# Feed-forward products whose moving operand is read alternately from two halves of a row

## Chip, core and metric

The kernel runs on one core of a Trainium2 chip. The metric is the device time of one execution in microseconds. A core has five engines with a queue of instructions each: TensorE (PE; its weight loads are listed apart as PEld), VectorE (DVE), ScalarE (ACT), GpSimd (POOL) and SyncE (SP), which here issues all transfers.

## What is computed

Per batch (8), attention over 8 heads of 576 positions in two forms, a pooled one over groups of 4 positions and a local one over a window of 7, which are added to x; then a low-rank mix over the positions and a feed-forward of width 2048 with a residual:

```python
x = out_up + out_local                    # 8 x 576 x 512, from q, k, v
h = x.transpose(0, 2, 1) @ U @ V          # U: 576 x 32, V: 32 x 576
u = x + h.transpose(0, 2, 1)
ch = np.maximum(u @ w_ch1, 0.0) @ w_ch2   # 512 -> 2048 -> 512
return (u + ch).astype(np.float32)
```

## The kernel before

Everything is kept transposed: channels on the 128 partitions, positions along the free axis. A batch is cut into two tiles of TN = 288 positions, and the feed-forward runs over 8 x 2 tiles x 16 slices `fc` of the hidden width: 256 steps. All numbers of weight, u and hidden activation are split into a high part (`W1H`, `W2H`, `uH`, `hH`) and a rest (`W1L`, `W2L`, `uL`, `hL`), and each product is made of three: high x high, high x rest, rest x high.

- `ffn1` of a step makes 12 products of 128 x 128 weights with 288 moving columns (4 channel chunks x 3) into one PSUM tile `ps_h` (L884). ScalarE takes the positive part as `hH` (L891) and VectorE the rest as `hL` (L892).
- `ffn2`, LAG = 3 steps later, makes 12 more (4 output chunks x 3), which accumulate in `acc0` to `acc3` over the 16 slices (L907). Behind the last slice of a tile GpSimd adds `uH` and `uL` into `o1` (L917), VectorE adds `acc` to it (L920), and `o1` goes out (L923).

So the feed-forward is 256 x 24 = 6144 products. Its input u comes from attention, which works on pairs of heads, four of them in a batch, 28 in batches 1 to 7: scores and pooled attention (L722, L715, L535, L548), local attention on GpSimd and VectorE (`Pt` L795, L789; `acc` L800), a transposed read back (`xT`, L834), the low-rank mix (`ps_hu` L844, `ps_u` L859, `xT` L862) and the split into `uH` (L865) and `uL` (L867). The u tiles have two buffers each, `xT` has four.

No order is written by hand. A planner (`Plan.run`) simulates the five engines with a duration for every operation and, on each engine, takes among what is ready the one with the lowest priority number; attention has 10 times the number of its head pair, the feed-forward 1000 and more. The order that comes out is fixed when the program is built, and each engine runs its own list in that order. The planner's duration of the 12 products of `ffn1` is `PH`, that of the 3 products of one output chunk in `ffn2` is `PF`, in microseconds:

```python
PH, PF = 1.587, 0.398
```

Of the kernel before, what the change touches and what calls it, by code (L numbers as in the profile page):

```python
# [16 lines left out]
ALU = mybir.AluOpType  # L17
# [34 lines left out]
class Plan:  # L52
# [6 lines left out]
    def buf(self, pool, shape, dt, name, tag=None, bufs=1):  # L59
        return Buf(self, pool, shape, dt, name, tag or name, bufs)  # L60

    def op(self, eng, dur, fn, r=(), w=(), prio=0.0, after=(), lat=None, move=0.0, at=0.0):
        o = Op()
        o.eng, o.dur, o.fn, o.prio, o.succ, o.ndep, o.ready = eng, dur, fn, prio, [], 0, at
        o.lat, o.move = LATENCY[eng] + SLACK * (SLACK_FROM <= prio < 1000) if lat is None else lat, move
        deps = set(after)
        bufs = []
        for k in r:
            b = k[0] if isinstance(k, tuple) else k
            bufs.append(b)  # L70
            if k in self.last_w:
                deps.add(self.last_w[k])
            self.readers.setdefault(k, []).append(o)
        for k in w:
            b = k[0] if isinstance(k, tuple) else k
            bufs.append(b)
            if k in self.last_w:
                deps.add(self.last_w[k])
            deps.update(self.readers.get(k, ()))
            self.readers[k] = []  # L80
            self.last_w[k] = o
        deps.discard(o)
        o.margin = MARGIN[eng] * (MARGIN_FROM <= prio < 1000 and any(d.eng != eng for d in deps))
        o.bufs = [b for b in dict.fromkeys(bufs) if isinstance(b, Buf)]
        for b in o.bufs:
            b.uses += 1
        for d in deps:
            d.succ.append(o)
        o.ndep = len(deps)
        self.ops.append(o)  # L90
        return o
# [108 lines left out]
def attn_mix_ffn_kernel(ctx: ExitStack, tc, q, kp, vp, qT, kT, v, U, Ub, V, w1, w2, mask, band, eye, pat, pool, vw, vn, ident, outT):  # L200
    nc = tc.nc
# [10 lines left out]
    TN = 288  # L212
# [4 lines left out]
    W1S, W2P, W2S = 2, 20, 1  # L217
    W1A, AT, W1B, W1C = 5, 25, 1.6, 15
    PW0 = 0.5
    PH, PF = 1.587, 0.398  # L220
    PWx = 0.5
    pw = lambda prio: PW0 if prio < 10 else PWx
    W1P = 20
# [11 lines left out]
    op, buf = plan.op, plan.buf  # L235
# [11 lines left out]
    def psum(pool, name, tag, bufs):  # L247
        return buf(pool, [128, 512], F32, name, tag, bufs)
# [7 lines left out]
    def dma(fn, r, w, prio, kb=295.0, issue=0.47, lat=1.3):  # L256
        late = (3.0 if r else 4.0) * (0.5 * (prio >= 50) + 0.5 * (prio >= 80))
        return op(SP, issue, fn, r, w, prio, move=0.01 + kb / 290.0, at=AT if prio >= 35 else 0.0, lat=lat + late)

    def dve(n, fn, r, w, prio, two_x=False):  # L260
        return op(DVE, ((n / 2 if two_x else n) + 65) / 960.0, fn, r, w, prio)

    def act(n, fn, r, w, prio, base=0.143):
        return op(ACT, n / 1200.0 + base, fn, r, w, prio)

    def pool_tt(n, fn, r, w, prio, ns=2.11, after=()):
        return op(POOL, 0.147 + n * ns / 1000.0, fn, r, w, prio, after)
# [10 lines left out]
    W2 = {}  # L278
# [28 lines left out]
    def kept_tile(shape, name, n=2):  # L307
        if name not in kept:
            kept[name] = [0, [Kept(early_pool.tile([128, *shape], F32, name=f"{name}{i}")) for i in range(n)]]
        r = kept[name]  # L310
        r[0] += 1
        return r[1][(r[0] - 1) % n]
# [5 lines left out]
    for _ in range(2):  # L318
        m = kept_tile([NS, 2, KW], "ms_b")
        op(POOL, 0.4, lambda m=m: nc.gpsimd.tensor_copy(  # L320
            out=m()[:, :, :, KL:KW].rearrange("p r h k -> p (r h) k"),
# [485 lines left out]
    def u_of(b, t):  # L807
        if (b, t) not in u_bufs:
            u_bufs[(b, t)] = (buf(ffn, [128, NDC, TN], F32R, "uH", bufs=2), buf(ffn, [128, NDC, TN], F32R, "uL", bufs=2))
        return u_bufs[(b, t)]  # L810
# [58 lines left out]
                [ufk, (uH, hp)], [(uL, hp)], prio)  # L869

    hbuf, accs, last_h = {}, {}, {}
    FIRST, FILL = -10.0, 1000.0

    def ffn1(s, i):
        b, t, fc = s
        uH, uL = u_of(b, t)
        ps = psum(ps_h, "ps_h", "h", 2)
        fs = slice(fc * 128, (fc + 1) * 128)

        def mm():  # L880
            n = 0
            for dc in range(NDC):
                for w, u in ((W1H, uH), (W1H, uL), (W1L, uH)):
                    nc.tensor.matmul(ps()[:, :TN], w[:, dc, fs], u()[:, dc, :],  # L884
                                     start=(n == 0), stop=(n == 3 * NDC - 1))
                    n += 1
        ur = [(uH, c) for c in range(NDC)] + [(uL, c) for c in range(NDC)]
        op(PE, PH, mm, ur + [f"W1_{fc}H", f"W1_{fc}L"] + ["late"] * (i >= 3), [ps], FILL + i)
        hH = buf(ffn, [128, TN], F32R, "hH", bufs=4)
        hL = buf(ffn, [128, TN], F32R, "hL", bufs=3)  # L890
        last_h[i] = act(TN, lambda: nc.scalar.activation(hH(), ps()[:, :TN], AF.Relu), [ps], [hH], FIRST, 0.05)  # L891
        dve(TN, lambda: nc.vector.scalar_tensor_tensor(  # L892
            hL(), ps()[:, :TN], 0.0, hH().bitcast(F32), op0=ALU.max, op1=ALU.subtract), [ps, hH], [hL], FIRST)
        hbuf[s] = (hH, hL)

    def ffn2(s, i):
        b, t, fc = s
        hH, hL = hbuf.pop(s)
        if fc == 0:
            accs[(b, t)] = [psum(ps_acc, f"acc{e}", f"acc{e}", 1) for e in range(NDC)]  # L900
        ac = accs[(b, t)]

        for e in range(NDC):
            def mm(e=e):
                es = slice(e * 128, (e + 1) * 128)
                for n, (w, hx) in enumerate((("H", hH), ("H", hL), ("L", hH))):
                    nc.tensor.matmul(ac[e]()[:, :TN], W2[w][:, fc, es], hx(),  # L907
                                     start=(fc == 0 and n == 0), stop=(fc == NFC - 1 and n == 2))
            op(PE, PF, mm, [hH, hL, f"W2_{fc}H", f"W2_{fc}L"], [ac[e]], FILL + i + LAG - 0.5)
        if fc == NFC - 1:  # L910
            uH, uL = u_of(b, t)
            for e in range(NDC):
                if e == NDC - 1:
                    o1 = buf(loc, [128, TN], F32, "o1", "o1b", 1)
                else:
                    o1 = buf(ffn, [128, CN], F32, "o1", "cT:o1", 3)
                pool_tt(TN, lambda e=e, o1=o1: nc.gpsimd.tensor_tensor(  # L917
                    out=o1()[:, :TN], in0=uH()[:, e, :].bitcast(F32), in1=uL()[:, e, :].bitcast(F32), op=ALU.add),
                    [(uH, e), (uL, e), f"W2_{NFC - 1}L"], [o1], FIRST, after=[last_h[i - 1]])
                dve(TN, lambda e=e, o1=o1: nc.vector.tensor_tensor(  # L920
                    out=o1()[:, :TN], in0=ac[e]()[:, :TN], in1=o1()[:, :TN], op=ALU.add),
                    [ac[e], o1], [o1], FIRST)
                dma(lambda e=e, o1=o1: nc.sync.dma_start(  # L923
                    out=outT[e * 128:(e + 1) * 128, b * S + t * TN:b * S + (t + 1) * TN], in_=o1()[:, :TN]),
                    [o1], [], FIRST, 150, lat=0.4)
# [46 lines left out]
    for i in range(len(steps) + LAG):  # L972
        if i < len(steps):
            b, t, fc = steps[i]
            if t == 0 and fc == 0 and b > 0 and b + 1 < B:
                attention(b + 1)
            ffn1(steps[i], i)
        if i >= LAG:
            ffn2(steps[i - LAG], i - LAG)
# [67 lines left out]
```

## Time and profile before

| | |
|---|---|
| time, median of 3 runs | 1036.33 us (1035.78 to 1036.66) |
| span of the profiled execution, first to last instruction | 1033.0 us |
| TensorE busy | 990.1 us (96%), weight loads 970.6 us |
| VectorE, ScalarE, GpSimd busy | 513.8, 389.5, 556.2 us |
| products of L884 and L907 | 6144, mean duration 295 to 302 ns |
| mean granted TensorE clock | 0.982 |

Of the profiled execution only the span is given; the median of the runs stands 3.3 us above it. In rows of groups the columns are line, engine, operation, what it writes and reads, shapes, count, then busy microseconds, mean nanoseconds of one, and the idle time of the engine ahead of them with what ended it. In rows of stages they are the stretch, its length, then busy microseconds and count of the engines (all five: PE, PEld, DVE, ACT, POOL; for one line of products: PE and PEld), granted clock, DMA share and GB/s. In rows of the timeline and the chain: start, length, engine, line, what, count. In rows of waits: who waited for whom, total microseconds, times, longest. Durations of consecutive products overlap, so what a product costs is read from the distance between starts.

### The profile page before, as it was taken

What the parts mean: (1) busy time and instruction counts of PE and PEld (TensorE: products, weight loads), DVE (VectorE), ACT (ScalarE), POOL (GpSimd) and SP (SyncE); (2) the same over time, 40 slices, a digit from 0 to 9 for tenths busy, and PEclk for the clock granted to TensorE, in tenths of its full rate; (3) what the DMA queues carried; (4) which work ended last, traced back from release to release, by engine and by line L of the source; (5) the groups of instructions that cost most, each with busy time, mean ns of one, the idle gap of its engine ahead of it and who ended that gap; (6) DMA issues with size and microseconds to landing.
All of it is one profiled execution on the core that took longest, in us unless ns stands there. A gap on an engine that the chain in (4) does not pass through costs nothing.

```text
span 1033.0 us, 26869 instructions
## 1 busy us (share of the span) xinstructions
PE 990.1 (96%) x10831; PEld 970.6 (94%) x10831; DVE 513.8 (50%) x1018; ACT 389.5 (38%) x1234; POOL 556.2 (54%) x567
## 2 busy tenths in 40 slices
PE   5787889999999999999999999999999999999998
PEld 4677888999999999999999999999999999999998
DVE  6677987655444447545454545445644424211111
ACT  4576454434333334443344332334443232111110
POOL 4854678595655666585665656567675605211010
PEclk9788999999999999999999999999999999999999
DMA  9867764545445456555444453465555231000000
GB/s 291 232 173 204 193 184 104 134 117 125 102 116 121 108 145 151 123 120 144 116 121 115 121 125 87 113 143 155 125 134 131 75 76 35 24 1 23 2 23 24
DMA packets 222612, 120.30 MB, mean 116 GB/s; under 512 B 175492, under 2 KB 198456, under 8 KB 222488
## 3 DMA queue, kind: packets, MB, share of 16 engines
q1 hardware_dynamic: 222488, 118.58, 45.4%
q8 instruction: 85, 1.39, 0.6%
q14 instruction: 39, 0.32, 0.1%
HBM read 87.78 MB, written 30.75 MB: 115 GB/s over the span
## 4 chain that ended last, share of the span: by engine, by line
PE 87%; DVE 6%; ACT 3%; issue 2%; DMA 1%; POOL 1%; SPq 0%; DVEq 0%; ACTq 0%
PE acc L907 38%; PE ps_h L884 37%; PE ps_a L548 3%; PE ps_b L715 2%; PE ps_hu L844 2%; DVE c L343 1%; DVE c L345 1%; PE ps_t L535 1%; PE ps_b L722 1%; DMA w2r<-in_W 1%; PE ps_u L859 1%; PE ps_v L427 1%; PE ps_a L480 1%; DVE c L341 1%; PE ps_ba L651 1%
## 5 line engine op out<-in xcount | busy, mean ns | idle before, releaser
L907 PE MATMUL acc<-hH,W2H 128*128 128x288 f32 x1024 | 309.4, 302 | 0.0
L884 PE MATMUL ps_h<-uH,W1H 128*128 128x288 f32 x1024 | 304.4, 297 | 0.3 <-ACT uH L865 0.3
L884 PE MATMUL ps_h<-uL,W1H 128*128 128x288 f32 x1024 | 303.2, 296 | 0.5 <-POOL uL L867 0.5
L907 PE MATMUL acc<-hH,W2L 128*128 128x288 f32 x1024 | 302.3, 295 | 0.8 <-POOL W2L L350 0.8
L907 PE MATMUL acc<-hL,W2H 128*128 128x288 f32 x1024 | 302.0, 295 | 0.0
L892 DVE SCALAR_TENSOR_TENSOR hL<-ps_h,hH 128x288 fp32r<-128x288 f32 x256 | 116.3, 454 | 373.1 <-ACT hH L891 372.4
L884 PE MATMUL ps_h<-uH,W1L 128*128 128x288 f32 x1024 | 301.8, 295 | 0.0
L795 POOL TENSOR_TENSOR Pt<-vl,at 128x896 f32<-128x896 f32 (+1 forms) x135 | 233.2, 1811 | 97.6 <-DVE acc L800 44.7
L891 ACT ACTIVATE hH<-ps_h 128x288 fp32r<-128x288 f32 x256 | 104.8, 409 | 436.0 <-PE ps_h L884 435.5
L884 PEld LDWEIGHTS ps_h<-uH,W1H 128*128 128x128 f32 x1024 | 193.4, 189 | 0.8 <-ACT uH L865 0.5
L884 PEld LDWEIGHTS ps_h<-uL,W1H 128*128 128x128 f32 x1024 | 193.4, 189 | 0.7 <-POOL uL L867 0.7
L884 PEld LDWEIGHTS ps_h<-uH,W1L 128*128 128x128 f32 x1024 | 193.7, 189 | 0.0
L907 PEld LDWEIGHTS acc<-hH,W2L 128*128 128x128 f32 x1024 | 192.7, 188 | 1.0 <-POOL W2L L350 1.0
L907 PEld LDWEIGHTS acc<-hH,W2H 128*128 128x128 f32 x1024 | 192.6, 188 | 1.1
L907 PEld LDWEIGHTS acc<-hL,W2H 128*128 128x128 f32 x1024 | 193.0, 188 | 0.0
L800 DVE TENSOR_REDUCE acc<-Pt 128x128 f32<-128x1024 f32 (+1 forms) x135 | 145.6, 1104 | 10.9 <-ACT Pt L789 4.6
L836 POOL TENSOR_TENSOR xL<-xL,xH 116x640 fp32r<-116x640 f32 x28 | 43.9, 1566 | 94.8 <-ACT xH L835 85.9
L867 POOL TENSOR_TENSOR uL<-xT,uH 128x288 fp32r<-128x288 f32 x56 | 44.3, 810 | 81.0 <-ACT uH L865 73.9
L917 POOL TENSOR_TENSOR o<-uH,uL 128x288 f32<-128x288 f32 x64 | 49.7, 820 | 53.2 <-DMA out_t<-o 53.2
L506 POOL TENSOR_TENSOR vr<-vr 72x256 f32<-72x256 f32 x54 | 41.0, 760 | 35.6 <-DMA vr<-in_v 32.7
L789 ACT ACTIVATE Pt<-ul 128x128 f32<-128x128 f32 (+1 forms) x135 | 48.7, 444 | 20.2 <-DVE acc L800 13.8
L740 ACT ACTIVATE se<-ps_b 96x114 f32<-96x114 f32 x108 | 38.5, 357 | 46.6 <-PE ps_b L715 29.3
(126 smaller groups left out, 1080.0 us busy)
## 6 DMA issues: line engine op xcount, KB each, us to landing
vl<-in_vp SPq DMA_DIRECT2D x54, 240.0 KB
out_t<-o SPq DMA_DIRECT2D x64, 144.0 KB
w1r<-in_W SPq DMA_DIRECT2D x16, 512.0 KB
w2r<-in_W SPq DMA_DIRECT2D x16, 512.0 KB
Y<-x_s SPq DMA_DIRECT2D x112, 72.0 KB
gT<-in_kT SPq DMA_DIRECT2D x27, 291.0 KB
xL<-x_s SPq DMA_DIRECT2D x28, 280.0 KB
gq<-in_qT SPq DMA_DIRECT2D x27, 288.0 KB
```

The costliest lines, as they stand in the source:

```text
L506: pool_tt(256, lambda x=x: nc.gpsimd.tensor_tensor(out=x()[:, :, 0:2, :], in0=x()[:, :, 0:2, :], in1=x()[:, :, 2:4, :], op=ALU.add), [x], ...
L740: act(n * KL, lambda p=ps[hh], se=se, n=n, rows=rows: nc.scalar.activation(se()[rows, 0:n].rearrange("p r k -> p (r k)"), p()[rows, 0:n * ...
L789: act(n * D, lambda n=n, ps=ps, Pt=Pt: nc.scalar.activation(Pt()[:, :n, :, 7], ul()[:, ps, :], AF.Copy), [ul], [(Pt, 1)], prio, 0.16)
L795: nc.gpsimd.tensor_tensor(out=Pt()[:, :n, :, 0:7].rearrange("p s d o -> p o s d"), in0=win, in1=at()[:, ps, :].rearrange("p s o -> p o s") ...
L800: dve(8.5 * n * D, lambda n=n, ps=ps, Pt=Pt: nc.vector.tensor_reduce(out=acc()[:, ps, :], in_=Pt()[:, :n], axis=AX.X, op=ALU.add), [(Pt, 0 ...
L836: pool_tt(640, lambda: nc.gpsimd.tensor_tensor(out=xL(), in0=xL().bitcast(F32), in1=xH().bitcast(F32), op=ALU.subtract), [xL, xH], [xL], prio)
L867: pool_tt(TN, lambda uH=uH, uL=uL, uf=uf: nc.gpsimd.tensor_tensor(out=uL()[:, hp, :], in0=uf(), in1=uH()[:, hp, :].bitcast(F32), op=ALU.su ...
L884: nc.tensor.matmul(ps()[:, :TN], w[:, dc, fs], u()[:, dc, :], start=(n == 0), stop=(n == 3 * NDC - 1))
L891: last_h[i] = act(TN, lambda: nc.scalar.activation(hH(), ps()[:, :TN], AF.Relu), [ps], [hH], FIRST, 0.05)
L892: dve(TN, lambda: nc.vector.scalar_tensor_tensor(hL(), ps()[:, :TN], 0.0, hH().bitcast(F32), op0=ALU.max, op1=ALU.subtract), [ps, hH], [hL ...
L907: nc.tensor.matmul(ac[e]()[:, :TN], W2[w][:, fc, es], hx(), start=(fc == 0 and n == 0), stop=(fc == NFC - 1 and n == 2))
L917: pool_tt(TN, lambda e=e, o1=o1: nc.gpsimd.tensor_tensor(out=o1()[:, :TN], in0=uH()[:, e, :].bitcast(F32), in1=uL()[:, e, :].bitcast(F32), ...
```

## The change

The moving operand of every feed-forward product is read through `turns`: column 0 of the first half of the 288, column 0 of the second half, column 1 of the first half, and so on; the halves start 144 words apart. The number of columns, the weights, the PSUM writes and the instructions stay. The hidden activation thus lies in PSUM and in `hH` and `hL` in the new order, `ffn2` reads it through the same view, and the last addition (L920, now L925) puts the columns back: it reads `acc` in order and reads and writes `o1` with 72 words between one element and the next. The planner's two durations are set to new values.

```diff
-    PH, PF = 1.587, 0.398
+    PH, PF = 1.47, 0.369
...
+    def turns(x):
+        return x.rearrange("p (a n) -> p n a", a=2)
...
-                    nc.tensor.matmul(ps()[:, :TN], w[:, dc, fs], u()[:, dc, :],
+                    nc.tensor.matmul(ps()[:, :TN], w[:, dc, fs], turns(u()[:, dc, :]),
...
-                    nc.tensor.matmul(ac[e]()[:, :TN], W2[w][:, fc, es], hx(),
+                    nc.tensor.matmul(ac[e]()[:, :TN], W2[w][:, fc, es], turns(hx()),
...
-                dve(TN, lambda e=e, o1=o1: nc.vector.tensor_tensor(
-                    out=o1()[:, :TN], in0=ac[e]()[:, :TN], in1=o1()[:, :TN], op=ALU.add),
+                o1v = lambda o1=o1: o1()[:, :TN].rearrange("p (b a m) -> p m b a", b=2, a=2)
+                dve(TN, lambda e=e, o1v=o1v: nc.vector.tensor_tensor(
+                    out=o1v(), in0=ac[e]()[:, :TN].rearrange("p (m b a) -> p m b a", b=2, a=2), in1=o1v(), op=ALU.add),
                     [ac[e], o1], [o1], FIRST)
```

Five lines are added, so what was L884, L892, L907, L917, L920 and L923 is now L888, L896, L911, L921, L925 and L928; L715 to L867 keep their numbers. Because of the two durations the planner's order changes on every engine. The place that the prediction speaks of is the start of a batch. VectorE's order around the `xT` rows (L862) of batch 6's last head pair, before:

```order
L920 TENSOR_TENSOR o_12026<-acc_11197,o_12026 128x288
L849 TENSOR_TENSOR stk<-ps_hu,stk 32x128
L800 TENSOR_REDUCE acc<-Pt 128x128
L892 SCALAR_TENSOR_TENSOR hL<-ps_h,hH 128x288
L862 TENSOR_TENSOR xT<-ps_u,xT 128x288 x2
L800 TENSOR_REDUCE acc<-Pt 128x128 x2
```

and now:

```order
L849 TENSOR_TENSOR stk<-ps_hu,stk 32x128
L800 TENSOR_REDUCE acc<-Pt 128x128 x2
L896 SCALAR_TENSOR_TENSOR hL<-ps_h,hH 128x288
L862 TENSOR_TENSOR xT<-ps_u,xT 128x288 x2
L800 TENSOR_REDUCE acc<-Pt 128x128
L766 SCALAR_TENSOR_TENSOR ms<-sc,mask_sb 128x63
L925 TENSOR_TENSOR o_12509<-acc_11850,o_12509 128x72x4
```

Before, the output row ahead of the `xT` rows is that of the first tile of batch 5, and 179 of the 192 steps ahead of batch 6 have their `hL` row above it; now the output row that follows is that of the second tile of batch 5, and all 192 stand above. Counted the same way on TensorE, the products of L884 and L907 that stand between the last `ps_u` (L859) of batches 1 to 7 and the batch's first L884 were 0, 42, 108, 180, 240, 321 and 300; now they are 0, 36, 36, 36, 36, 36 and 24.

GpSimd's order at the same place, the split into `uL` (L867) for batch 6, before:

```order
L867 TENSOR_TENSOR uL<-xT,uH 128x288 x3
L836 TENSOR_TENSOR xL<-xL,xH 116x640
L413 TENSOR_TENSOR smq<-gh 128x144
L411 TENSOR_TENSOR gh<-gT 128x288
L413 TENSOR_TENSOR smk<-gh 128x144
```

and now:

```order
L921 TENSOR_TENSOR o_12550<-uH,uL 128x288
L795 TENSOR_TENSOR Pt<-vl,at 128x7x128
L867 TENSOR_TENSOR uL<-xT,uH 128x288 x5
L795 TENSOR_TENSOR Pt<-vl,at 128x7x64
L506 TENSOR_TENSOR vr<-vr 72x2x128
```

Before, the first tile's `uL` was made for three pairs together, for the last pair some rows later and for the second tile later still; now the last pair's and the second tile's four are made in one go, behind the additions of the batch ahead.

## Prediction

> **What bounds the kernel now.** I read the page first (busy shares, the slices, the chain that ended last), then the costliest groups by shape, then the busy time by stage, and last single rows of the timeline for the distance between two products.
>
> ```profile
> PE 990.1 (96%) x10831; PEld 970.6 (94%) x10831; DVE 513.8 (50%) x1018; ACT 389.5 (38%) x1234; POOL 556.2 (54%) x567
> PE   5787889999999999999999999999999999999998
> PEclk9788999999999999999999999999999999999999
> ...
> PE 87%; DVE 6%; ACT 3%; issue 2%; DMA 1%; POOL 1%; SPq 0%; DVEq 0%; ACTq 0%
> PE acc L907 38%; PE ps_h L884 37%; PE ps_a L548 3%; PE ps_b L715 2%; PE ps_hu L844 2%; DVE c L343 1%; DVE c L345 1%; PE ps_t L535 1%; PE ps_b L722 1%; DMA w2r<-in_W 1%; PE ps_u L859 1%; PE ps_v L427 1%; PE ps_a L480 1%; DVE c L341 1%; PE ps_ba L651 1%
> ```
>
> The feed-forward products (L884 and L907) alone are 75% of the chain that ended last. By stage, with what these two lines do ahead of 226 us and behind it (two answers, one for each line):
>
> ```profile
> 200.00:300.00 100.00, 99.23 (x1060) 98.02 (x1060) 47.07 (x97) 37.46 (x121) 64.61 (x68) 1.00 0.52 128
> 300.00:800.00 500.00, 500.00 (x5617) 495.38 (x5616) 256.20 (x517) 197.38 (x661) 314.42 (x325) 1.00 0.52 124
> 800.00:1000.00 200.00, 200.00 (x1625) 199.76 (x1624) 54.53 (x117) 40.55 (x113) 47.38 (x47) 1.00 0.13 34
> ```
>
> ```profile
> 0.00:226.00 226.00, 60.67 (x394) 56.32 (x394) 0.92 0.66 182
> 226.00:1033.00 807.00, 391.47 (x2678) 366.48 (x2678) 1.00 0.41 98
> ...
> 0.00:226.00 226.00, 58.41 (x384) 53.27 (x384) 0.92 0.66 182
> 226.00:1033.00 807.00, 405.53 (x2688) 369.51 (x2688) 1.00 0.41 98
> ```
>
> From 300 to 1000 us TensorE never idles, at full granted clock, while POOL, the next in load, is busy 63% of 300 to 800 us. Behind 226 us lie 2678 + 2688 = 5366 of these products; ahead of it 394 + 384 = 778, at a lower mean clock (0.92).
>
> What one product occupies is not its duration (295 ns, overlapped) but the distance to the next. From the chain's last stretch, then the timeline at three places: half clock, two x5 groups of 128 columns at full clock, and five weight loads back to back (PEld):
>
> ```profile
> 1000.13 1.58 PE ps_h L884 x12
> ...
> 1023.96 4.80 PE acc L907 x36
> 97.23 0.44 PE L884 MATMUL ps_h<-uH,W1L 128*128 128x288 f32 x1
> 97.47 0.44 PE L884 MATMUL ps_h<-uH,W1H 128*128 128x288 f32 x1
> 690.98 0.47 PE L844 MATMUL ps_hu<-xH,Ust 116*64 116x128 f32 x5
> 691.28 0.46 PE L844 MATMUL ps_hu<-xL,Ust 116*64 116x128 f32 x5
> 59.71 0.53 PEld L639 LDWEIGHTS ps_bt<-ident_sb,ms_b 128*128 128x128 f32 x5 [0.17 <-issue]
> ```
>
> Between 1000.13 and 1023.96 stand 15 pieces of 12 products: 23.83 us / 180 = 132.4 ns each, at full clock. At half clock the same product takes 97.47 - 97.23 = 240 ns. Half of 240 is 120, so 12.4 ns of the 132.4 did not shrink with the clock. How much of that is fixed? The 128-column products lie (691.28 - 690.98) / 5 = 60 ns apart: per column (132.4 - 60) / 160 = 0.4525 ns, fixed part 2.1 ns. So about 10 ns of every 288-column product is a slowdown per column that is absent at half clock: something that feeds or drains the array does not keep up. The weight load is not it, since five loads of 128 columns take 0.53 us, at most 106 ns each.
>
> **The change, part by part.**
>
> *Products, 6144 of them (L884, L907).* Same columns, same weights, other read order. Nothing in the trace reads a moving operand so. Floor: 120 ns from the half-clock row plus the fixed 2.1, 122.1 ns, which is also above the 106 of the weight loads. Ceiling: 132.4 plus a line-crossing price, worked out under the rivals. I take 122.5. The reason for the lower end is not only that it is the nearest row of this very product, but the planner's numbers: before, PH / 12 = 132.25 and PF / 3 = 132.7, which are the 132.4 of the trace to 0.3%, so that table has held distances as the chip gives them; the new ones, 1.47 / 12 = 122.5 and 0.369 / 3 = 123, lie 0.4 ns above the floor that the two clocks give. Saving 9.9 ns each.
>
> Behind 226 us TensorE is the bound, and nothing else runs on the path: 5366 x 9.9 = **-53.1 us**. Ahead of it 778 x 9.9 = 7.7 us, of which part only makes TensorE wait: the second batch's u arrives late already, and the other engines there convert weights. Ends 0 and 7.7, taken half: **-3.8**.
>
> *The waits at the batches' starts.* Batch 1 starts with its u just arriving:
>
> ```profile
> 225.26 0.40 PE L884 MATMUL ps_h<-uH,W1H 128*128 128x288 f32 x1 [0.30 <-ACT uH L865]
> 226.13 0.40 PE L884 MATMUL ps_h<-uL,W1H 128*128 128x288 f32 x1 [0.47 <-POOL uL L867]
> ...
> 221.48 0.46 PE L844 MATMUL ps_hu<-xH,Ust 116*64 116x128 f32 x5
> 881.48 0.47 PE L844 MATMUL ps_hu<-xH,Ust 116*64 116x128 f32 x5
> 923.72 0.29 PE L884 MATMUL ps_h<-uH,W1H 128*128 128x288 f32 x1
> ```
>
> Its wait is 0.77 us, and it is the only one behind 200 us. Later batches had slack: the last batch's u was begun at 881.48 and first used at 923.72. In the new order (shown above) that slack is gone: every batch from the second on has its last pair's u just ahead of its first step, as batch 1 has. Six more such starts at 0.4, between 0 and 0.77, cost **+2.5**. That attention keeps up at all I take from these rows:
>
> ```profile
> DVE hL L892 <- ACT hH L891: 372.4, 183, 3.3
> ...
> ACT hH L891 <- PE ps_h L884: 435.5, 210, 3.9
> ```
>
> VectorE and ScalarE stand 372 and 436 us in front of feed-forward steps that TensorE has not finished; attention's work is queued behind these steps, so shorter steps release it sooner. That idle time is the cover for attention; the rival below prices its loss.
>
> *The last addition (L920, now scattered in SBUF).* 64 additions; their cost in the middle is covered by the 372 us. Only the last four are on the path:
>
> ```profile
> 1027.62 0.46 DVE L920 TENSOR_TENSOR o<-acc,o 128x288 f32<-128x288 f32 x1 [2.72 <-PE acc L907]
> 1028.38 1.19 DVE L920 TENSOR_TENSOR o<-acc,o 128x288 f32<-128x288 f32 x3 [0.30 <-PE acc L907]
> L920 DVE TENSOR_TENSOR o<-acc,o 128x288 f32<-128x288 f32 x64 | 26.2, 450 | 19.3 <-PE acc L907 19.1
> L339 ACT ACTIVATE c<-w1r 128x512 f32<-128x512 f32 x16 | 10.6, 667 | 0.0
> L347 ACT ACTIVATE W1H<-c 128x512 fp32r<-128x512 f32 x16 | 10.1, 629 | 3.0 <-DVE c L345 2.9
> L789 ACT ACTIVATE Pt<-ul 128x128 f32<-128x128 f32 x108 | 40.0, 472 | 9.4 <-DMA ul<-up_s 5.8 <-DVE acc L800 3.1
> L789 ACT ACTIVATE Pt<-ul 128x64 f32<-128x64 f32 x27 | 8.9, 329 | 10.8 <-DVE acc L800 10.7
> L800 DVE TENSOR_REDUCE acc<-Pt 128x128 f32<-128x1024 f32 x108 | 128.4, 1211 | 10.9 <-ACT Pt L789 4.6 <-POOL Pt L795 4.1 <-issue 1.6
> L800 DVE TENSOR_REDUCE acc<-Pt 128x64 f32<-128x512 f32 x27 | 18.2, 675 | 0.0
> ```
>
> L789 writes one word in eight: (472 - 329) / 64 = 2.23 ns an element. L800 reads in order on VectorE: (1211 - 675) / 512 = 1.05 ns. A scattered addition is bounded by 450 ns (no penalty) and 450 + 288 x (2.23 - 1.05) = 790 ns. Four in a row from 1027.62 then end at 1030.8 instead of 1029.57 at worst. Neither row is near it (another engine, another stride), so the middle: **+0.6**.
>
> *Sum.* 1033.0 - 53.1 - 3.8 + 2.5 + 0.6 = 979.2 us of span. The runs' median, 1036.33, stands 3.3 above the profiled span; with the same 3.3 the time is 982.5, rounded to **983 us**.
>
> [...] L339 reads every second word and takes 667 ns where L347 reads all of them in 629: 38 ns more for 512, 0.074 ns an element. [...]
>
> **The rivals.**
> - *Every column pays a line (slower).* Place: L884 and L907. The mildest price is that of L339: 0.074 x 288 = 21 ns, 153.4 a product. All 6144 pay, since TensorE would be the bound everywhere: 6144 x 21 = 129 us, **1165 us**. The price of L789 (1.2 ns over contiguous) would triple the time of a product. It decides against me from the first distance above 132.4. For it: those two rows. Against: the planner's numbers.
> - *The read is not what lags (no change).* If the array's output or a clash with the weight loads costs the 10 ns, the order of reading changes nothing: 1036 plus up to 3 from the tight starts and the additions, **1036 to 1039**. For it: PEld is busy 94% of the time and loads beside every product. Against: 106 ns a load.
> - *Attention becomes the pace.* If it does not speed up with the steps, the last u is begun at 881.48 still, and is ready 226.13 - 221.48 = 4.65 us later; then 768 products of the last batch, 94.1 us, and the 4.2 us from 1028.8 to the end, 0.6 more for the additions: 985.0, **988 us**, and up to 1004 where the new order also delays it. For it: no slack left in the order. Against: the 372 and 436 us.
> - *Half the lag goes.* 127.5 ns: half of 56.9 us, **1010 us**.
>
> **How the numbers follow.** Full rate with TensorE as the bound, 0.62 (974 to 990: all of 6144 x 9.9 = 60.8 saved gives 975.5, none of the early part and 3 more of waits gives 990); attention as the pace 0.12; half 0.08; no change 0.07; slower read 0.11. Faster by over 0.2% (what a measurement of this kernel can tell, about 2 us): 0.62 + 0.12 + 0.08 = 0.82. Of the no-change case most stays within 0.2%: 0.05; the rest and the slower read: 0.13. The range 974 to 1012 leaves out the last two cases and little else.
>
> **What would show it.** Right: 12 products of L888 (the old L884) in 1.47 us at full clock; rows of L911 123 ns apart; L859, unchanged, still 132 apart; TensorE without idle time from 300 us on but for tenths at the batches' starts; the waits of ACT for ps_h well below 436 us. Wrong: a distance of 132 or more; or TensorE waiting several us for uL at each batch's start; or attention's last pair still at 881 us.

## The result and the profile after

The changed kernel takes 989.32 us (median of 4 runs, 986.86 to 992.23) against 1036.49 us: a ratio of 0.954, interval 0.9515 to 0.9565. That is 4.6% faster, 6 us above the forecast of 983 and inside its range. The profiled execution took 992.23 us with a span of 990.4 us, so it is the slowest of the four; in every execution the time stands some 1.8 us above the span.

From the page of the changed kernel: the busy shares, the rows of the 40 slices for TensorE and its clock, and the chain that ended last:

```profile
PE 937.6 (95%) x10831; PEld 917.0 (93%) x10831; DVE 517.8 (52%) x1018; ACT 389.4 (39%) x1234; POOL 539.9 (55%) x567
PE   5787798998999999999999999999999999999998
PEclk9778799998999999999999999999999999999999
PE 81%; DVE 11%; ACT 3%; issue 2%; DMA 2%; POOL 1%; SPq 0%; DVEq 0%; ACTq 0%; POOLq 0%
PE ps_h L888 34%; PE acc L911 34%; PE ps_a L548 3%; DVE acc L800 2%; PE ps_b L715 2%; DVE c L343 2%; PE ps_hu L844 1%; DVE o L925 1%; PE ps_t L535 1%; PE ps_v L427 1%; DVE c L345 1%; PE ps_b L722 1%; PE ps_a L480 1%; DVE hL L896 1%; DVE c L341 1%
```

TensorE is still the bound, but two small things are new. VectorE's share of the chain went from 6% to 11%, and `hL` (L896) now appears in it. And in the tenth slice (223 to 248 us), where the clock was at 9 tenths or more before, it is at 8. By stage, and two pieces of the chain's last stretch:

```profile
200.00:300.00 100.00, 96.17 (x1061) 94.37 (x1061) 53.51 (x103) 41.51 (x138) 67.12 (x70) 0.97 0.55 128
300.00:800.00 500.00, 495.32 (x5818) 490.40 (x5817) 256.17 (x520) 199.34 (x665) 304.55 (x324) 1.00 0.53 122
...
965.86 1.47 PE ps_h L888 x12
982.03 4.06 PE acc L911 x33
```

Twelve products now take 1.47 us, 122.5 ns each, where they took 1.58 to 1.59. The products of L859, which are read in order in both kernels, stand 132 ns apart before and 135 now, so the gain goes with the read. From 300 to 800 us TensorE loses 4.7 us, which it did not before. The waits behind 235 us are one row, and it is not the one that the prediction feared (`uL`). It is a PSUM buffer `ps_h` that VectorE has not yet emptied into `hL`. The rows of TensorE, VectorE and ScalarE at the start of batch 2:

```profile
PE ps_h L888 <- DVE hL L896: 4.7, 5, 0.9
...
343.24 0.29 PE L888 MATMUL ps_h<-uH,W1L 128*128 128x288 f32 x1
344.45 0.39 PE L888 MATMUL ps_h<-uH,W1H 128*128 128x288 f32 x1 [0.93 <-DVE hL L896]
...
339.85 0.66 DVE L925 TENSOR_TENSOR o<-acc,o 128x288 f32<-128x288 f32 x1
340.54 1.79 DVE L925 TENSOR_TENSOR o<-acc,o 128x288 f32<-128x288 f32 x3
343.41 0.63 DVE L800 TENSOR_REDUCE acc<-Pt 128x64 f32<-128x512 f32 x1
343.95 0.45 DVE L896 SCALAR_TENSOR_TENSOR hL<-ps_h,hH 128x288 fp32r<-128x288 f32 x1
...
342.49 0.26 ACT L772 ACTIVATE ms<-ms 128x63 f32<-128x63 f32 x1 [3.79 <-DVE ms L769]
```

Four scattered additions of the tile ahead, then attention's rows, stand in VectorE's queue before the batch's first `hL`. ScalarE stands still with it: its attention row L772 waits 3.79 us for a row of VectorE behind the additions, and the batch's first `hH` is queued behind L772. The same wait of 0.93 to 0.95 us returns at 455.8, 567.0, 678.4 and 789.9 us, the starts of batches 3 to 6. The group of the additions (busy, mean ns) shows 657 ns where the additions in order took 450 before:

```profile
L925 DVE TENSOR_TENSOR o<-acc,o 128x288 f32<-128x288 f32 x64 | 38.7, 657 | 6.2 <-PE acc L911 6.1
```

The start of batch 1 is worse. TensorE's rows there, then TensorE alone by stretch (busy, granted clock, DMA share, GB/s), the first three of the changed kernel and the last three of the kernel before:

```profile
224.57 0.51 PE L844 MATMUL ps_hu<-xL,Ust 116*64 116x128 f32 x5 [2.10 <-POOL xL L836]
226.03 0.53 PE L859 MATMUL ps_u<-Vst,stk 128*128 128x288 f32 x2 [0.95 <-DVE stk L849]
229.64 0.61 PE L888 MATMUL ps_h<-uL,W1H 128*128 128x288 f32 x1 [0.56 <-POOL uL L867]
230.04 0.45 PE L888 MATMUL ps_h<-uH,W1L 128*128 128x288 f32 x1
230.28 0.45 PE L888 MATMUL ps_h<-uH,W1H 128*128 128x288 f32 x1
```

```profile
220.00:226.40 6.40, 3.18 (x28) 1.00 0.29 93
226.40:230.00 3.60, 3.00 (x13) 0.55 0.00 0
230.00:233.50 3.50, 3.50 (x16) 0.50 0.80 232
```

```profile
220.00:226.40 6.40, 5.63 (x46) 1.00 0.31 99
226.40:230.00 3.60, 3.60 (x37) 1.00 0.85 253
230.00:233.50 3.50, 3.50 (x113) 1.00 0.34 69
```

Before, the two halves of `ps_hu` ran back to back and nine feed-forward products stood between them and `ps_u`; TensorE waited at neither place. In the new order the products are used up earlier, TensorE waits 2.10 us for `xL` between the two halves and 0.95 us ahead of `ps_u`, and it is busy for only 3.18 of 6.40 us. Then its granted clock falls to half (0.55, then 0.50) for some 7 us: products are 240 ns apart (230.04, 230.28). The longest single gap ahead of that is 2.10 us.

### The profile page after: what moved, and what is told of

Read it like the earlier page. It is cut to its first block, busy times and chain, and to the rows that moved or that the text cites. A ratio compares the mean times of both kernels' runs of the same rounds, so it can differ in the third digit from the quotient of the medians.

```text
span 990.4 us, 26862 instructions
## 1 busy us (share of the span) xinstructions
PE 937.6 (95%) x10831; PEld 917.0 (93%) x10831; DVE 517.8 (52%) x1018; ACT 389.4 (39%) x1234; POOL 539.9 (55%) x567
## 4 chain that ended last, share of the span: by engine, by line
PE 81%; DVE 11%; ACT 3%; issue 2%; DMA 2%; POOL 1%; SPq 0%; DVEq 0%; ACTq 0%; POOLq 0%
PE ps_h L888 34%; PE acc L911 34%; PE ps_a L548 3%; DVE acc L800 2%; PE ps_b L715 2%; DVE c L343 2%; PE ps_hu L844 1%; DVE o L925 1%; PE ps_t L535 1%; PE ps_v L427 1%; DVE c L345 1%; PE ps_b L722 1%; PE ps_a L480 1%; DVE hL L896 1%; DVE c L341 1%
## 5 line engine op out<-in xcount | busy, mean ns | idle before, releaser
L888 PE MATMUL ps_h<-uH,W1H 128*128 128x288 f32 x1024 | 297.9, 291 | 4.7 <-DVE hL L896 4.7
L911 PE MATMUL acc<-hH,W2H 128*128 128x288 f32 x1024 | 299.8, 293 | 0.0
L888 PE MATMUL ps_h<-uL,W1H 128*128 128x288 f32 x1024 | 295.0, 288 | 0.6 <-POOL uL L867 0.6
L888 PE MATMUL ps_h<-uH,W1L 128*128 128x288 f32 x1024 | 294.8, 288 | 0.0
L911 PE MATMUL acc<-hH,W2L 128*128 128x288 f32 x1024 | 293.6, 287 | 0.7 <-POOL W2L L350 0.7
L911 PE MATMUL acc<-hL,W2H 128*128 128x288 f32 x1024 | 293.3, 286 | 0.0
L896 DVE SCALAR_TENSOR_TENSOR hL<-ps_h,hH 128x288 fp32r<-128x288 f32 x256 | 116.5, 455 | 332.4 <-ACT hH L895 331.3
L795 POOL TENSOR_TENSOR Pt<-vl,at 128x896 f32<-128x896 f32 (+1 forms) x135 | 218.9, 1691 | 114.9 <-DVE acc L800 59.1
L888 PEld LDWEIGHTS ps_h<-uH,W1H 128*128 128x128 f32 x1024 | 195.3, 191 | 7.1 <-DVE hL L896 5.8
L888 PEld LDWEIGHTS ps_h<-uL,W1H 128*128 128x128 f32 x1024 | 195.4, 191 | 0.9 <-POOL uL L867 0.9
L888 PEld LDWEIGHTS ps_h<-uH,W1L 128*128 128x128 f32 x1024 | 195.4, 191 | 0.0
L911 PEld LDWEIGHTS acc<-hH,W2L 128*128 128x128 f32 x1024 | 194.0, 189 | 1.1 <-POOL W2L L350 1.1
L911 PEld LDWEIGHTS acc<-hH,W2H 128*128 128x128 f32 x1024 | 194.1, 190 | 0.4
L911 PEld LDWEIGHTS acc<-hL,W2H 128*128 128x128 f32 x1024 | 194.1, 190 | 0.0
L921 POOL TENSOR_TENSOR o<-uH,uL 128x288 f32<-128x288 f32 x64 | 49.0, 796 | 49.5 <-DMA out_t<-o 49.5
L867 POOL TENSOR_TENSOR uL<-xT,uH 128x288 fp32r<-128x288 f32 x56 | 43.7, 801 | 21.3 <-ACT uH L865 21.3
L789 ACT ACTIVATE Pt<-ul 128x128 f32<-128x128 f32 (+1 forms) x135 | 46.2, 421 | 14.0 <-DVE acc L800 13.7
```

The costliest lines, as they stand in the source:

```text
L789: act(n * D, lambda n=n, ps=ps, Pt=Pt: nc.scalar.activation(Pt()[:, :n, :, 7], ul()[:, ps, :], AF.Copy), [ul], [(Pt, 1)], prio, 0.16)
L795: nc.gpsimd.tensor_tensor(out=Pt()[:, :n, :, 0:7].rearrange("p s d o -> p o s d"), in0=win, in1=at()[:, ps, :].rearrange("p s o -> p o s") ...
L867: pool_tt(TN, lambda uH=uH, uL=uL, uf=uf: nc.gpsimd.tensor_tensor(out=uL()[:, hp, :], in0=uf(), in1=uH()[:, hp, :].bitcast(F32), op=ALU.su ...
L888: nc.tensor.matmul(ps()[:, :TN], w[:, dc, fs], turns(u()[:, dc, :]), start=(n == 0), stop=(n == 3 * NDC - 1))
L896: dve(TN, lambda: nc.vector.scalar_tensor_tensor(hL(), ps()[:, :TN], 0.0, hH().bitcast(F32), op0=ALU.max, op1=ALU.subtract), [ps, hH], [hL ...
L911: nc.tensor.matmul(ac[e]()[:, :TN], W2[w][:, fc, es], turns(hx()), start=(fc == 0 and n == 0), stop=(fc == NFC - 1 and n == 2))
```

## The experiments

### Which read orders are fast

One kernel, in the planner's new durations, with another read order in each of the 16 tiles; `turns` splits the 288 columns into streams `s` words apart. It leaves out putting the columns back:

```diff
+    ORDERS = [1, 1, 1, 144, 72, 48, 36, 24, 18, 16, 12, 8, 4, 2, "pairs", "fours"]
+    def turns(x, k):
+        s = ORDERS[k]
...
+        if s in ("pairs", "fours"):
+            return x.rearrange("p (a n w) -> p n a w", a=2, w=2 if s == "pairs" else 4)
+        return x.rearrange("p (a n) -> p n a", n=s)
```

> One order of reading per tile of 288 positions, in ffn1 and ffn2 alike; the columns' order is not restored, so output columns of these tiles come out permuted. Tile 2 reads in order; tiles 3 to 13 read with a stride of 144, 72, 48, 36, 24, 18, 16, 12, 8, 4 and 2 words; tile 14 takes 2 columns and tile 15 takes 4 columns from each half in turn, the halves 144 words apart. Theory A (successive columns out of the same 16-byte neighbourhood are what lags): every stride of 4 words and more gives 122.5 ns a product, stride 2 and tile 14 lie between, tile 15 near 132. Rival B (two sequential streams are what helps, and more streams cost a line each): 122.5 for stride 144 and tile 14 only, the small strides at 132 or above, up to 153. In-order tile: 132.4 by both.

Measured, as the median distance between two products inside a tile:

| streams (distance in words) | ns a product |
|---|---|
| in order | 132 |
| 2 (144) | 122.5 |
| 4 (72) | 153 |
| 6 (48) | 167 |
| 8 (36), 12 (24), 16 (18), 18 (16) | 247 to 252 |
| 24 (12) | 326 |
| 36 (8), 72 (4), 144 (2) | 245, 261, 257 |
| two streams, 2 columns from each in turn | 186 |
| two streams, 4 columns from each in turn | 136 |

Pieces of 12 from the chain: in order, 144, 72, 36 and 12 words apart, and the two forms with 2 and 4 columns in turn; then TensorE alone by stretch (busy, granted clock, DMA share, GB/s) ahead of the tile with 24 streams and inside it:

```profile
276.39 1.59 PE ps_h L895 x12
330.91 1.47 PE acc L918 x12
396.54 1.84 PE ps_h L895 x12
562.53 2.97 PE ps_h L895 x12
1009.93 3.91 PE ps_h L895 x12
1400.12 2.23 PE ps_h L895 x12
1440.84 1.63 PE ps_h L895 x12
...
880.00:900.00 20.00, 20.00 (x88) 1.00 0.14 44
1000.00:1020.00 20.00, 20.00 (x63) 0.50 0.00 0
```

What follows: of these orders, two streams alone are faster than in order (122.5 ns); more streams cost much (153 to 326). Both expectations missed: theory A had every distance from 4 words up at 122.5 ns, and rival B had two columns in turn at 122.5 and nothing above 153. Two columns in turn from each stream are slower (186) than one (122.5). In the tile with 24 streams the granted clock was at half from 1000 to 1020 us (0.50) although TensorE never idled there (20.00 of 20.00 us). The piece of 12 at 1009.93 (3.91 us, 326 ns each) is from that stretch; what this read takes at full clock is not shown. That the prediction's price for "every column pays a line" (153.4 ns, from a row of ScalarE) is just what four streams cost is chance, but a slower read was a real danger.

### How far apart two streams must be

The same, with always two streams, in blocks, `d` words apart; here too the columns are not put back:

```diff
+    DISTANCES = [144, 144, 144, 72, 48, 36, 24, 18, 16, 12, 9, 8, 6, 4, 3, 2]
+    def turns(x, k):
+        return x.rearrange("p (c a n) -> p c n a", a=2, n=DISTANCES[k])
```

> Two streams in every tile, at another distance in each: columns are read alternately from two neighbouring blocks of d words, block pair after block pair; tiles 0 to 2 use d = 144, tiles 3 to 15 use 72, 48, 36, 24, 18, 16, 12, 9, 8, 6, 4, 3 and 2 words. The columns' order is not restored, so the output columns come out permuted. Theory (two lines can be held open, and the lag of reading in order comes from the change to the next line): 122.5 to 124 ns at every d of 4 words and more, a little more at small d where both lines change more often. Rival (the two streams must lie in different banks, and the distance decides): some distances, those that are multiples of 16 or 8 words, at 150 and above, others at 122.5. [...]

Measured: 144, 72, 48, 36, 24, 18, 16, 12, 8, 6 and 4 words all give 122.5 ns; 9 words give 132, 3 give 154, and 2 give 132, as in order. The chain's pieces at 9, 4, 3 and 2 words:

```profile
720.24 1.59 PE acc L913 x12
871.25 1.47 PE ps_h L890 x12
939.50 1.84 PE acc L913 x12
990.03 1.58 PE ps_h L890 x12
```

What follows: the distance need not be large. All even distances tried from 4 words up are fast (122.5 ns); 2 words and the two odd ones tried, 3 and 9, are not (132, 154 and 132). So the rival that some multiples of 8 or 16 words are slow falls, and the theory, which had 9 words at 122.5 to 124, does not explain the odd ones. That the memory is read by lines or banks, as the expectations suppose, no run here shows.

### Is it the read, the weight load or the output?

In order again, with `ffn1` alone in another form in each tile:

```diff
+    FORMS = ["", "", "", "w64", "n144", "turns", "turns w64", "turns n144", "same", "bf16"] + [""] * 6
...
+                    if form == "same":
+                        x = x[:, 0:1].broadcast_to([128, TN])
...
+                        parts = [(slice(fc * 128, fc * 128 + 64), slice(0, 64), slice(0, TN), x)]
```

> The order of the kernel before, with another form of the ffn1 products in each of seven tiles, so the output is not the reference's: tile 3 uses 64 weight columns in 10 of 12 products; tile 4 splits these 10 into two of 144 columns; tile 5 reads alternately; tile 6 alternately with 64 weight columns; tile 7 alternately and split; tile 8 takes all columns from one word; tile 9 takes the upper 2 bytes of each word as bf16, weights too. Theory A (the moving read alone lags, per column): tile 3 stays at 132.4, tile 4 gives 67 per half (2.1 + 144 x 0.4525), tiles 5 and 6 122.5, tile 7 62. Rival C (the moving read clashes with the weight load): tile 3 falls to about 127, tile 6 stays at 122.5. Tile 8 tells whether one line read again and again lags: 132 or above by A, 122.5 if leaving a line is what costs. Tile 9: 122.5 if bytes matter, 132 if the line matters.

Measured: with 64 weight columns instead of 128, in order, the distance stays at 132 ns; all 288 columns read from one word give 122.5; the alternate read gives 122.5 with 128 weight columns and with 64; products of 144 columns come 112 to 114 ns apart in either order (pieces of 22 in 2.50 us in order and 2.48 alternately, with 2 products of 288 columns among the 22), not 67 and 62 as expected. That is near the 106 ns of a weight load in the rows before, which may be the floor there; no run separates it. The upper 16 bits of both operands alone, read with a step of 4 bytes, take 128 ns at the median (a piece of 12 took 1.56 us, 130 each). `ffn2`, in order throughout, stays at 133. Pieces at 64 weight columns in order, 144 columns in order (22 products), one word, and alternate:

```profile
330.06 1.57 PE ps_h L906 x12
356.08 2.50 PE ps_h L906 x22
630.60 1.47 PE ps_h L906 x12
432.85 1.47 PE ps_h L906 x12
```

What follows: half the weight columns, and with them half the output rows, change nothing, and another address order, with the same weights and the same PSUM writes, takes the 10 ns away. They lie in reading the moving operand in order.

### Read and durations apart

The read alone (old durations) and the durations alone (read in order):

```diff
-    PH, PF = 1.47, 0.369
+    PH, PF = 1.587, 0.398
```

> The alternate reading with the old two durations, so the order of the kernel before on every engine. Theory (what is missing to 983 is lost by the new order: no slack at the batches' starts, and the longer way to the first product): 982 to 985, no waits of TensorE behind 230 us but tenths. Rival (the early part is bound by attention and weights in either order, and the waits come from the scattered addition): within 1.5 us of the changed kernel, 988 to 991. A third: feed-forward steps run ahead of what the old order assumed and wait for u: above 992.

```diff
-    PH, PF = 1.587, 0.398
+    PH, PF = 1.47, 0.369
```

> Reading in order, as before, with the two new durations alone, so the order of the changed kernel on every engine. Theory (the order alone costs a few us, since TensorE is the bound and only the slack is gone): 1036 to 1042. Rival (the order is worth a part of the gain): 1025 to 1034.

Measured: the read alone 985.42 us, ratio 0.9485 (0.9466 to 0.9503); the durations alone 1044.5 us, 1.0046 (1.0026 to 1.0066). The changed kernel, run again, is the third corner:

> The changed kernel again, on the chip of the next two: 0.954 of the kernel before by every theory, some 989 to 992 us.

It gave 989.86 us, 0.9522 (0.9488 to 0.9556). So the read is worth 5.2%. The durations, though nearer to the truth, cost some 0.4 to 0.5%: with the read in order the interval excludes no change, and the 1044.5 us lie above the 1042 that was expected; with the alternate read the two intervals overlap. The kernel with the durations alone shows the half clock at the start of batch 1 too, with the read in order:

```profile
231.00:237.50 6.50, 5.55 (x23) 0.51 0.45 125
```

It has no wait for `hL` at the later batches, and the kernel with the read alone has neither the half clock there nor those waits.

### Which durations cost it

Old durations for the first 64 steps (batches 0 and 1) and new ones behind, then the reverse (`i >= 64`):

```diff
-        op(PE, PH, mm, ur
+        op(PE, 1.587 if i < 64 else PH, mm, ur
...
-            op(PE, PF, mm, [hH
+            op(PE, 0.398 if i < 64 else PF, mm, [hH
```

> The changed kernel with the planner's old durations for the first 64 steps (batches 0 and 1) and the new ones behind. Theory 1 (the new order loses ahead of batch 1's first step: the first product 4 us later, u of batch 1 later): 4 to 5 us below the repeated changed kernel, first product at 78.5, the 0.93 us waits at the batches' starts stay. Theory 2 (it loses at the starts of the later batches): within 1.5 us of the repeated changed kernel.

> The other half: new durations for the first 64 steps, the old ones from batch 2 on. Theory 1: within 2 us of the repeated changed kernel, first product at 82 to 84 us. Theory 2: 4 to 6 us below it, without the 0.93 us waits.

Measured: old ones early 983.83 us, 0.9465 (0.9436 to 0.9495), with no wait behind 235 us; old ones late 987.59 us, 0.9505 (0.9475 to 0.9535). The intervals of these two overlap, so that most of the loss is made in the first two batches is likely, not shown. The traces agree with it: old ones late keep the half clock at the start of batch 1 (221.5 to 228.3 us) and one of the five waits (0.93 us, batch 2); old ones early have neither. So an order begun otherwise does not have the later waits either, which theory 1 had staying. It was wrong on the first product too, which came at 82.5 us with the old durations early and at 78.3 with them late, the reverse of what was expected.

### What makes the later waits

The changed kernel with the last addition in order, so that the orders of all engines stay and only the additions' length changes; it leaves out putting the columns back:

```diff
-                o1v = lambda o1=o1: o1()[:, :TN].rearrange("p (b a m) -> p m b a", b=2, a=2)
-                dve(TN, lambda e=e, o1v=o1v: nc.vector.tensor_tensor(
-                    out=o1v(), in0=ac[e]()[:, :TN].rearrange("p (m b a) -> p m b a", b=2, a=2), in1=o1v(), op=ALU.add),
+                dve(TN, lambda e=e, o1=o1: nc.vector.tensor_tensor(
+                    out=o1()[:, :TN], in0=ac[e]()[:, :TN], in1=o1()[:, :TN], op=ALU.add),
```

> The changed kernel with its last addition (L925) in order, as before the change: the output's columns stay in the changed order. TensorE's order and every other engine's are those of the changed kernel. In that kernel TensorE waits 0.93 to 0.95 us at the start of batches 2 to 6 for a ps_h buffer that VectorE still has to empty into hL (4.7 us in all), and four additions of 657 ns stand in VectorE's queue ahead of that hL. Theory C (the scattered additions make these waits): an addition falls to about 450 ns, hL comes 4 x 0.207 = 0.83 us earlier, the five waits shrink to 0.1 us each, idle time behind 226 us falls from 4.7 to about 0.6, and the time to about 985.5 against 989.5 of the changed kernel (ratio to before 0.948). Rival D (the waits come from the order of VectorE's queue and ScalarE's round trips in attention, not from the additions' length): additions 450 ns, waits still 0.6 us or more each, time within 1.5 us of the changed kernel.

Measured: 985.83 us, 0.9474 (0.9447 to 0.9502). The five waits shrank to 0.11 to 0.12 us each; TensorE's idle time behind the start of batch 1 is 0.57 us. Four additions shorter by 0.2 us each took 0.82 us off each wait, so the scattered additions made them. Not all of the time need be theirs: the half clock at the start of batch 1 lasted 3.4 us in this execution, 6.8 in the changed kernel's, which is worth an estimated 1.6 us (14 products of 117.5 ns more).

The planner reckons 0.368 us for such an addition. With 0.69:

```diff
-                dve(TN, lambda e=e, o1v=o1v: nc.vector.tensor_tensor(
+                op(DVE, 0.69, lambda e=e, o1v=o1v: nc.vector.tensor_tensor(
```

> The changed kernel with the planner's duration of the last addition (L925) set from 0.368 to 0.69 us, about what the trace shows (657 ns). Only VectorE's order and a little of the others' change. Theory C2 (the planner placed hL behind the additions because it took them to be short): hL moves ahead of some additions or is released earlier, the 0.93 us waits at the starts of batches 2 to 6 mostly go, time 985 to 987 (ratio 0.949). Rival D2 (the additions have the lowest priority number on VectorE and go first whatever they last): the waits stay at 0.9 us, time 989 to 990 (0.953).

Measured: 983.05 us, 0.9459 (0.9436 to 0.9483), no wait behind 235 us (one of 0.83 us for `hL` stands at 233.8, in batch 1), and the clock full from 222 to 233 us. The rival, that the planner puts additions first whatever they last, falls. The time came out 2 us better than the 985 to 987 expected; that had reckoned with the later waits alone, and the other order also spared the half clock.

### The same read, 4 words apart

```diff
     def turns(x):
-        return x.rearrange("p (a n) -> p n a", a=2)
+        return x.rearrange("p (c a n) -> p c n a", a=2, n=4)
```

with the last addition's views made to match (`"p (c b a m) -> p c m b a"`, m = 2).

> The changed kernel with the two streams 4 words apart (columns 0,4,1,5,2,6,3,7, then the next eight) in place of 144; the last addition puts the columns back within each eight. Orders of all engines as in the changed kernel. From the kernel with many distances: products 122.5 ns apart in the middle of each tile, so the same 61 us are saved. Open is the last addition: if its extra 207 ns come from jumping 72 words between elements, it falls to 450 to 520 ns and with it the waits at the batch starts, time about 986; if they come from any access that is not one after the other, it stays at 650 ns or more and the time at 989 to 990. If the time is above 995, distance 4 is not at full rate over a whole kernel.

> The last kernel (streams 4 words apart) with the planner's old durations for the first 64 steps (batches 0 and 1) and the new ones behind, the best plan so far (0.9465 of before with streams 144 words apart). Expected 982 to 985 (ratio 0.945 to 0.947), 4 to 6 us below the changed kernel, with idle time behind 226 us of 0.5 us or less and some 92 products of 213 ns in place of 117. If the gain of that plan came only from hiding the additions' length, the kernels with streams 4 words apart and with 144 apart differ by less than 1 us here.

Measured: with the new durations 987.35 us, 0.9491 (0.9472 to 0.9511); with the old ones early 981.54 us, 0.9441 (0.9419 to 0.9462), the fastest version here. The additions' group in the first kernel, TensorE at the start of batch 2 in it, and then the additions' group and two stages of the second:

```profile
L925 DVE TENSOR_TENSOR o<-acc,o 128x288 f32<-128x288 f32 x64 | 25.6, 445 | 6.2 <-PE acc L911 6.1
```

```profile
342.60 0.29 PE L888 MATMUL ps_h<-uH,W1L 128*128 128x288 f32 x1
342.99 0.39 PE L888 MATMUL ps_h<-uH,W1H 128*128 128x288 f32 x1
```

```profile
L925 DVE TENSOR_TENSOR o<-acc,o 128x288 f32<-128x288 f32 x64 | 26.0, 450 | 24.3 <-PE acc L911 21.6 <-POOL Pt L795 2.5
```

```profile
226.40:230.00 3.60, 3.51 (x35) 1.00 0.87 245
300.00:800.00 500.00, 500.00 (x5968) 495.89 (x5966) 256.20 (x539) 207.76 (x692) 316.78 (x335) 1.00 0.54 126
```

With jumps of a few words an addition takes 445 to 450 ns, as in order, and the waits at the batches' starts are down to 0.10 to 0.11 us. So the extra 207 ns were the jumps of 72 words, and the column order can be put back at no cost. In the first kernel the clock still falls behind the start of batch 1 (0.51 from 226.0 to 232.7 us). In the second it stays at 1.00, and TensorE is busy for all of 300 to 800 us; that this makes the whole distance of 5.8 us is likely, not shown. Against 144 words with the same plan, 4 words gave 0.9441 instead of 0.9465; the intervals overlap, so a gain on that plan is not shown.

## Why the prediction was right, and where its terms were off

- **Products: right.** 122.5 ns was forecast from the half-clock row, the fixed part and the planner's numbers, and 122.5 was measured (means of 132.4 and 122.5 at full clock). Some 6000 of the 6144 distances fell by 9.9 ns, 59.4 us in all; the terms behind and ahead of 226 us had 60.8 together. The others stand mostly at half clock or beside attention blocks. That another order would lift the lag rested on the planner's new numbers alone; no row of the kernel before could tell it, and the read orders and forms measured since are what shows it.
- **Ahead of the start of batch 1: wrong.** I took -3.8, half of the products' 7.7. What happened is -7.7 for the products, +4.9 of idle time from the first product to the start of batch 1, and about +2.6 for some 22 products at half clock (22 x 117.5 ns): nothing was left. That part of the gain would turn into waiting was foreseen, and 0 was one end of the forecast; the half clock had no term. The step that failed was to look for the new waits at batches 2 to 7 and take batch 1 as it was.
- **Waits at the later batches: wrong in cause, and half the size.** +2.5 was forecast, for late `uL`; 4.7 was measured, for `ps_h` held by `hL`, five times 0.94. The prediction put the starts of the later batches on a par with batch 1, but there no product stands between the last `ps_u` and the first step, and at the later ones 36 do (24 at batch 7), 4.4 us of work: in batch 2 the first tile's last `uL` is done at 337.56 us and its first step begins at 340.42. The source of the real waits is the additions' length, which the prediction had covered with VectorE's 372 us of idle time. That time is a sum over the whole span; four additions in a row at one place are not covered by it.
- **The last addition on the path: about right.** 657 ns lies inside the bounds of 450 and 790, near the middle that was taken. From the last product's start to the end of the span it is 4.5 us before, 4.3 after and 3.9 in the kernel with the additions in order. So the scattered additions cost 0.4 us by the last pair, near the +0.6; against the profile before the end moved by -0.2, because the time behind the last addition was longer there (3.4 us, then 2.7), which no run here explains.
- **The first product's start** came 4.4 us later in the profiled execution (78.2, then 82.5 us), which I had no term for. It does not go with the change: it was 80.2 in the repeat of the changed kernel and 78.3 to 84.8 over the other kernels. It goes with the clock granted around it: from 50 to 85 us that was 0.90 in the three profiles with a start at 78.2 to 78.5, and 0.79 in the one with 84.8. Before and after from 50 to 85 us:

```profile
50.00:85.00 35.00, 30.00 (x533) 26.75 (x530) 28.40 (x53) 24.70 (x68) 16.49 (x14) 0.90 0.58 167
50.00:85.00 35.00, 29.18 (x428) 25.54 (x427) 24.66 (x49) 23.88 (x70) 17.02 (x18) 0.82 0.51 146
```

- **Span to time.** I added 3.3 us, the distance of the median from one profiled span. The time of one execution is its span plus 1.8, as the runs since show; the other 1.5 was that execution's luck.

The sum for the profiled span: 4.4 - 59.4 + 4.9 + 2.6 + 4.7 - 0.2 = -43.0, against 990.4 - 1033.0 = -42.6. The medians lie 47.2 us apart, since the profiled execution was a fast one before and the slowest one after; without the 4.4 of the first product the sum is -47.4. The forecast had -53.3. The 6 us that are missing are in the main the early part (3.8) and the later waits (2.2 more than forecast).

Of the rivals, that the read is not what lags fell with the read from one word and the alternate read, and its clash with the weight load with the 64 weight columns; a price for every column shows from four streams on, not for two; and the lag went whole, not by half. The line-crossing price, of the ceiling as of the rival with a price for every column, was worked out from ScalarE's L339 (0.074 ns an element); that a line is crossed no run shows, and what the runs showed in its place is 122.5 ns with two streams and 153 with four. Attention as the pace would have given 988, close to the measured time, but not by its mechanism: behind 235 us TensorE waits for no `u` at all, and the last batch's `u` stands in the order with products on both sides:

```profile
886.86 0.47 PE L844 MATMUL ps_hu<-xH,Ust 116*64 116x128 f32 x5
888.99 0.43 PE L859 MATMUL ps_u<-Vst,stk 128*128 128x288 f32 x2
892.19 0.29 PE L888 MATMUL ps_h<-uH,W1H 128*128 128x288 f32 x1
```

The sign that I named for it, the last pair still at 881 us, was a poor one. It came at 886.86, because the new order puts that pair behind more products (5340 of them, 5040 before), not because attention was slow. The other sign did what I said: ScalarE's waits for `ps_h` fell from 436 to 349 us, by 87, more than the products save; where the rest comes from is not shown.

```profile
ACT hH L895 <- PE ps_h L888: 349.0, 191, 3.6
```

## What to carry to other kernels

When the busiest engine's distance between instructions stands above what its rows at half clock allow (here 132.4 ns against half of 240), suspect the addresses that it reads, and try another order of the same data; with the streams 4 words apart it cost nothing here but views (the addition took 445 to 450 ns, 450 in order). Try several: every order of more than two streams measured here is slower than reading in order (153 to 326 ns against 132). An engine's idle time over the span covers no burst (VectorE's 372 us did not cover four additions of 657 ns in a row): before a step is called hidden, look at what stands behind it in its queue at the places where the bound engine waits for that queue. And durations that are nearer to the truth for one operation can make a planned order worse (ratio 1.0046 with the read in order). For the later waits the reason is another duration that was still wrong (the addition at 0.368 for 0.657 us); the loss at the start of batch 1 comes with the additions in order too, and its reason is open.

## What the runs showed of the hardware beyond what was expected

- A product of 128 x 128 weights with 288 moving columns reads 9.9 ns slower in order (132.4) than from two streams (122.5) or from a single word (122.5). Two streams take 122.5 at every even distance tried from 4 to 144 words; 9 words give 132, 3 give 154 and 2 give 132 ns. Why odd distances and the order itself cost time is not settled; no run here tells it.
- More than two streams cost 153 (four) to 326 ns (24). The piece of 326 stood at half the granted clock; at full clock it is not shown.
- VectorE's addition of 128 x 288 takes 657 ns with jumps of 72 words and 445 with jumps inside 8 words, 450 in order.
- TensorE's clock fell to half behind a stretch of 6.4 us in which TensorE was busy for 3.18 us, with no single gap above 2.10 us, and it stood at half through a stretch in which TensorE never idled (24 streams, 0.50 from 1000 to 1020 us). Where it falls differs between kernels with like gaps: the kernel told 0.69 us had gaps of 1.72 and 1.16 us there and kept the full clock (1.00 from 222 to 233 us).
